# First layer of a two-layer Hedgehog-attention and Mish kernel: six blocks' normalized rows are turned by VectorE and reloaded from DRAM by features; the first stage's products run by kinds

## The chip, the cores and the metric

The kernel runs on one NeuronCore of one Trainium2 chip. The metric is the device time of one execution in microseconds (us), lower is better. Engines are named TensorE (PE in the profile, with PEld for its weight loads), VectorE (DVE), ScalarE (ACT), GpSimd (POOL) and SyncE (SP, which issues the DMAs). PSUM is the memory that TensorE writes; the other tiles lie in SBUF.

## What is computed

Two equal layers over x of 2048 rows and 640 features, in fp32. The layers share their weights.

```python
x = A_x                                           # (1, 2048, 640)
for layer in range(2):
    x = x + A(layernorm(x)) ; x = x + B(layernorm(x))

def A(x):                                         # linear attention, 32 heads of 20
    q, k, v = split(x @ wqkv)
    pq, pk = q @ w_phi, k @ w_phi                 # per head, 20 x 20
    phi = concat(softmax(p), softmax(-p))         # of pq and of pk, 40 wide
    kv, z = phi_k^T v, sum over rows of phi_k
    return ((phi_q kv) / (phi_q z + 1e-6)) @ wo
def B(x):                                         # 640 -> 1536 -> 640
    h = x @ w1 + b1
    return (h * tanh(softplus(h))) @ w2
```

## The kernel before

The 2048 rows are cut in NB = 8 blocks of 256 rows, each of BT = 2 tiles of 128 rows; NT = 16 tiles in all. A product in fp32 precision is made of three TensorE matmuls in a rounded format (fp32r): every operand is kept as a high part (ScalarE copies it to the rounded format) and a low part (VectorE subtracts the high part from the original), and high x high, high x low and low x high are accumulated in PSUM.

Each layer has three stages. The first stage (`attend_first`) makes queries, keys and values of every tile and accumulates phi_k^T [v, 1] over all rows. The second stage (`attend_second`) applies that to the queries, multiplies by wo, adds the result to the rows and takes their statistics. The third (`dense`) is the Mish layer.

The change lies in the first stage. Its matmuls need the normalized rows with the features on the partitions, that is transposed. In the first layer, `fetch_normed(b)` loads a block of rows (line 384), takes mean and variance (`norm_stats`, VectorE lines 250 and 252; `norm_scale`, GpSimd lines 259 and 260, VectorE line 262), `normed` writes the normalized rows to two row tiles (ScalarE, by `act`), and `Transposed.step` turns them on TensorE: a block has 5 x 2 squares of 128 x 128, ten transposes through PSUM (line 280). The same `step` then makes high and low parts (lines 285 and 286; three steps of four, four and two squares). In the second layer the end of `dense` has already normalized the rows; `spill_turned` transposes them on VectorE within 32 x 32 blocks (line 315) and writes them with eight DMAs of 80 KB (line 317) to a DRAM tensor laid out by features, n2_d; `fetch_normed` there only calls `load_turned`, three loads into row tiles (line 325), and `step` makes the parts straight from these tiles, without TensorE. `dense` gets its own inputs by the same route, through n1_d.

For each tile there are three products of 30 matmuls (line 344): keys, queries and values, written k0, q0, v0 for the block's first tile and k1, q1, v1 for its second. `order` gives their sequence, by blocks. Each is a generator: its first part computes the product and moves it out of PSUM, and each later call of `advance`, once per product, takes every pending generator one part further, newest first. For keys the parts are:

- right after the product: ScalarE moves it out of PSUM to a "big" tile
- one product later: VectorE takes maxima and minima (line 368, two), and makes both differences (lines 369 and 371)
- two later: ScalarE's exponential
- three later: VectorE's sums and reciprocals (lines 377 and 378), GpSimd's scaling (line 379)
- five later: 22 matmuls accumulate phi_k^T [v, 1] (line 414)

Queries go the same way, with line 369 on GpSimd, into a tile of their own ring ("r" in the profile, two tiles); four products later VectorE transposes them in 32 x 32 blocks (line 423) and four DMAs of 160 KB write them to e_d, by features (line 427). Values are only moved out of PSUM.

Between the products of block b, at index n of the order, block b+1 is prepared: at n = 0 `fetch_normed(b + 1)`, at n = 2 `normed`, and at n = 3, 4 and 5 one `step` each.

A scheduler orders the instructions of every engine from this program by a simulated timeline; `act` ties ScalarE's instructions of this stage in program order. Buffers: product tiles in PSUM ("mm") 2, other PSUM tiles ("one") 4, "big" 5, rows ("xt") 2, row tiles ("xn") 4, values ("v") 2.

Of the kernel before, what the change touches and what calls it, by code (L numbers as in the profile page):

```python
# [18 lines left out]
D = 640  # L19
# [5 lines left out]
BT = 2  # L25
# [17 lines left out]
def kernel(  # L43
# [56 lines left out]

    e_d = [dram.tile([EW, BLK], F32, name=f"e_d{b}") for b in range(NB)]

    n1_d = [dram.tile([D, BLK], F32, name=f"n1_d{b}") for b in range(NB)]
    n2_d = [dram.tile([D, BLK], F32, name=f"n2_d{b}") for b in range(NB)]
    x1_d = dram.tile([S, D], F32, name="x1_d")
# [140 lines left out]
    def norm_stats(t, xt):  # L246

        bn = work.tile([P, 2, 6], F32, tag="bn", name="bn", bufs=2)
        for c in range(2):
            nc.vector.bn_stats(bn[:, c], xt[:, t, c * HC:(c + 1) * HC])  # L250
        mv = work.tile([P, 2], F32, tag="mv", name="mv", bufs=3)
        nc.vector.bn_aggr(mv, bn)
        return mv

    def norm_scale(b, mvs):

        ve = work.tile([P, BT], F32, tag="ve", name="ve", bufs=2)
        for t in range(BT):
            nc.gpsimd.tensor_scalar(ve[:, t:t + 1], mvs[t][:, 1:2], LN_EPS, 1.0, op0=ALU.add, op1=ALU.mult)
        nc.gpsimd.tensor_tensor(stats[:, b, 0], ve, neg_half, op=ALU.pow)  # L260
        for t in range(BT):
            nc.vector.scalar_tensor_tensor(stats[:, b, 1, t:t + 1], mvs[t][:, 0:1], -1.0,
                                           stats[:, b, 0, t:t + 1], op0=ALU.mult, op1=ALU.mult)
# [35 lines left out]
    def normed(b, xt):  # L299

        xn = [row_tile() for _ in range(BT)]
        for t in range(BT):
            act(xn[t], xt[:, t, :], AF.Identity,
                                 bias=stats[:, b, 1, t:t + 1], scale=stats[:, b, 0, t:t + 1])
        return Transposed(xn)
# [13 lines left out]
    def load_turned(src, tiles):  # L319

        cols = []
        for c, make in zip(range(0, KD, 2), tiles):
            n = min(2, KD - c)
            cols.append(make()[:, :n * BLK].rearrange("p (k s) -> p k s", k=n))
            nc.sync.dma_start(cols[-1], src[c * P:(c + n) * P].rearrange("(k p) s -> p k s", p=P))
        return Transposed(cols=cols)
# [55 lines left out]
    def fetch(x_src, b, xt=None):  # L382
        xt = x_tile() if xt is None else xt
        nc.sync.dma_start(xt, row_block(x_src, b))
        return xt

    def attend_first(layer, x_src, first):


        def fetch_normed(b):  # L390
            if layer:
                return load_turned(n2_d[b], [row_tile] * 3)
            xt = fetch(x_src, b)
            norm_scale(b, [norm_stats(t, xt) for t in range(BT)])
            return xt

        pending = []

        def advance():
            for g in pending[::-1]:  # L400
                try:
                    next(g)
                except StopIteration:
                    pending.remove(g)

        def keys(xts, i, v):
            e = big_tile()
            yield from features(project(xts, i % BT, kv_ws, 0), e, False)
            yield
            for g in range(G):  # L410
                p, n = divmod(g, 2)
                w, m = (120, 64) if g < 10 else (80, 42)
                acc, c = (kva, 120 * p) if p < 4 else (kvz, 120 * (p - 4))
                nc.tensor.matmul(acc[64 * n:64 * n + m, c:c + w], v[:, GW * g:GW * g + m],  # L414
                                 e[:, 120 * g:120 * g + w],
                                 start=(i == 0 and p in (0, 4)), stop=(i == NT - 1),
                                 skip_group_check=True)

        def queries(xts, i, ps=None):
            e = query_tile(i)  # L420
            yield from features(project(xts, i % BT, q_ws, 0) if ps is None else ps, e, True)

            nc.vector.transpose(e, e)
            b, t = divmod(i, BT)
            dst = e_d[b].rearrange("(j f) (t q s) -> t q f j s", f=32, t=BT, s=32)
            for q in range(4):
                nc.sync.dma_start(dst[t, q], e[32 * q:32 * q + 32].rearrange("f (j s) -> f j s", s=32))
                if b == NB - 1:
                    yield

        def values(xts, i, v):
            vv = v.rearrange("p (h d) -> p h d", d=DH + 1)
            act(vv[:, :, DH], ident[:, :H], AF.Copy, scale=0.0, bias=1.0)
            if i < BT:
                pv = project(xts, i, kv_ws, D, [one_tile(), one_tile()])
                for c in range(2):
                    act(vv[:, c * H // 2:(c + 1) * H // 2, :DH],
                        pv[c][:, :HC].rearrange("p (h d) -> p h d", d=DH), AF.Copy)
            else:
                pv = project(xts, i % BT, kv_ws, D)  # L440
                act(vv[:, :, :DH].rearrange("p (c h) d -> p c h d", c=2),
                    both(pv).rearrange("p c (h d) -> p c h d", d=DH), AF.Copy)
            yield

        if first is None:
            with tc.manual_schedule(engines={mybir.EngineType.SP}):
                bd = big_tile()[:120, :720].rearrange("p (t c) -> p t c", t=6)
                nc.sync.dma_start(bd[:, :3], phi_bd[:, :3])
                raw = load_raw(0, range(3))
                xt = fetch_normed(0)  # L450
                nc.sync.dma_start(bd[:, 3:], phi_bd[:, 3:])
                raw += load_raw(0, range(3, 6))
                nxt = normed(0, xt).all()
                q_ws = [r2_pair(k) for k in range(KD)]
                fold_phi(q_ws, bd, raw)
                kv_ws = load_v_weights()
                raw = load_raw(1)
            nc.sync.dma_start(mask, head_mask)
        else:
            nxt, kv_ws = first  # L460
            q_ws = load_q_weights()
        for b in range(NB):
            xts = nxt
            order = ("k0", "v0", "q0", "k1", "v1", "q1")
            if b == 0:
                order = ("v0", "q0", "v1", "k0", "q1", "k1")
            elif b == 1:
                order = ("k0", "q0", "k1", "v0", "q1", "v1")
            elif b == NB - 1:
                order = ("k0", "k1", "v0", "v1", "q0")  # L470
            vs = [v_tile() for _ in range(BT)]
            for n, (kind, t) in enumerate(order):
                t = int(t)
                i = b * BT + t
                if b == 0 and n == 1:
                    if layer:
                        load_k_weights(kv_ws)
                if b == 0 and n == 3:
                    if layer == 0:
                        fold_phi(kv_ws, bd, raw)  # L480
                    kva, kvz = one_tile(), one_tile()
                if b == NB - 1 and n == 3:
                    loaded = {0: load(0)}
                if b + 1 < NB:
                    if n == 0:
                        xt = fetch_normed(b + 1)
                    elif n == 2:
                        nxt = xt if layer else normed(b + 1, xt)
                    elif n > 2:
                        nxt.step()  # L490
                g = {"k": lambda: keys(xts, i, vs[t]), "q": lambda: queries(xts, i),
                     "v": lambda: values(xts, i, vs[t])}[kind]()
                next(g)
                advance()
                pending.append(g)
            if b == 1:
                if layer == 0:
                    spill_qk_weights(kv_ws, q_ws)
                o_ws = load_o_weights()

        def rest():

            ps = [one_tile(), one_tile()]
            project_half(ps[0], xts, 1, q_ws, 0, 0)
            advance()
            advance()
            yield
            project_half(ps[1], xts, 1, q_ws, 0, 1, range(3))
            yield
            project_half(ps[1], xts, 1, q_ws, 0, 1, range(3, KD))  # L510
            pending.append(queries(xts, NT - 1, ps))
            next(pending[-1])
            while pending:
                yield
                advance()

        return kva, kvz, o_ws, loaded, rest()
# [379 lines left out]
```

## Time and profile before

| | us |
|---|---|
| median of 3 runs (1401.17 to 1402.03) | 1401.89 |
| the profiled execution | 1400.33 |
| its span, first to last instruction | 1398.6 |
| TensorE busy | 1384.2 |
| VectorE busy | 1074.5 |
| ScalarE busy | 584.1 |
| GpSimd busy | 442.3 |
| granted TensorE clock | 1.000 |

The profile names an instruction by its line in the kernel, its engine, its operation and `out<-in` by the program's tile names. In a table of groups, "x4 | 3.0, 801 | 0.4 <-ACT" means four instructions, 3.0 us busy in all, 801 ns for one on average, and 0.4 us in which the engine stood idle before them, ended by ScalarE. A row of a timeline is start, duration, engine, line, operation and the number of instructions merged in it. A row of waits names who waited for whom, the total, the number of times and the longest. A row of the chain of waits is start, length, engine, line and count. Consecutive matmuls overlap in the pipeline, so their distance from start to start is shorter than one's duration.

The first layer's first stage runs until about 281 us, its blocks 1 to 6 from 53 to 237 us; the second layer's first stage lies around 715 to 960 us.

### The profile page before, as it was taken

The page shows a single profiled execution, that of the slowest core. Times are in us where ns is not written, and L with a number is a line of the kernel's source. Part 1 is how long each engine was busy: PE and PEld are TensorE (multiplying, and loading weights), DVE is VectorE, ACT ScalarE, POOL GpSimd, SP SyncE. Part 2 cuts the span into 40 slices and gives each one's busy share as a digit, 9 for nine tenths or more (in the row PEclk, how much of TensorE's full clock was granted, in tenths as well). Part 3 has the DMA queues.
Part 4 walks back from the last instruction along what each step waited for, and adds up shares of the span by engine and source line. Part 5 has one row for each costly group of instructions (what it writes and reads, how often), then busy time and mean ns, then how long its engine had stood idle before and what let it go on. Part 6 is the DMA issues. An engine that isn't in the chain of part 4 may idle for free. (4 is left out here: it accounts for less than half of the span.)

```text
span 1398.6 us, 28120 instructions
## 1 busy us (share of the span) xinstructions
PE 1384.2 (99%) x11528; PEld 1367.6 (98%) x11528; DVE 1074.5 (77%) x1820; ACT 584.1 (42%) x973; POOL 442.3 (32%) x334
## 2 busy tenths in 40 slices
PE   7999999999999999999999999999999999999998
PEld 7999999999999999999999999999999999999998
DVE  5798877696698877788769887887767876767775
ACT  4444344321355454545454333332234444444443
POOL 1354444343422222222234443433352211211112
PEclk9999999999999999999999999999999999999999
DMA  8533422689733423343374333357976212333200
GB/s 319 169 79 57 75 40 39 185 237 292 254 87 95 111 75 64 91 114 95 106 273 89 71 65 69 50 109 218 288 251 208 69 26 77 95 95 95 73 24 20
DMA packets 350035, 169.57 MB, mean 121 GB/s; under 512 B 286866, under 2 KB 323458, under 8 KB 349906
## 3 DMA queue, kind: packets, MB, share of 16 engines
q1 hardware_dynamic: 349906, 167.78, 44.2%
q8 instruction: 90, 1.47, 0.4%
q14 instruction: 39, 0.32, 0.1%
HBM read 104.82 MB, written 62.91 MB: 120 GB/s over the span
## 5 line engine op out<-in xcount | busy, mean ns | idle before, releaser
L735 PE MATMUL mm<-r2h,ol 128*128 128x320 f32 x1280 | 304.7, 309 | 0.0
L719 POOL TENSOR_TENSOR ol<-big,ol 128x512 fp32r<-128x512 f32 (+1 forms) x98 | 129.8, 1325 | 484.1 <-ACT ol L718 407.8
L693 PE MATMUL one<-xtl,r1h 128*128 128x256 f32 x960 | 268.2, 279 | 0.0
L693 PE MATMUL one<-xth,r1l 128*128 128x256 f32 x960 | 268.0, 279 | 0.0
L693 PE MATMUL one<-xth,r1h 128*128 128x256 f32 x960 | 265.9, 279 | 0.0
L735 PEld LDWEIGHTS mm<-r2h,ol 128*128 128x128 f32 x1280 | 219.1, 188 | 0.0
L735 PE MATMUL mm<-r2l,ol 128*128 128x320 f32 x640 | 197.3, 309 | 0.0
L344 PE MATMUL mm<-r1h,xth 128*128 128x320 f32 x600 | 188.3, 314 | 0.0
L344 PE MATMUL mm<-r1h,xtl 128*128 128x320 f32 x600 | 185.7, 310 | 0.7 <-DVE xtl L286 0.7
L344 PE MATMUL mm<-r1l,xth 128*128 128x320 f32 x600 | 185.6, 309 | 0.0
L693 PEld LDWEIGHTS one<-xtl,r1h 128*128 128x128 f32 x960 | 180.4, 188 | 0.0
L693 PEld LDWEIGHTS one<-xth,r1l 128*128 128x128 f32 x960 | 180.4, 188 | 0.0
L693 PEld LDWEIGHTS one<-xth,r1h 128*128 128x128 f32 x960 | 179.6, 188 | 0.0
L708 DVE TENSOR_SCALAR big<-big 128x512 f32<-128x512 f32 (+1 forms) x98 | 56.4, 575 | 110.7 <-ACT big L706 110.5
L379 POOL TENSOR_TENSOR r<-r,r 128x1280 f32<-128x1280 f32 x32 | 75.8, 2367 | 142.6 <-DVE r L378 136.8
L735 PEld LDWEIGHTS mm<-r2l,ol 128*128 128x128 f32 x640 | 120.2, 188 | 0.0
L710 ACT ACTIVATE big<-big,two 128x512 f32<-128x512 f32 (+1 forms) x98 | 70.1, 715 | 116.1 <-DVE big L709 116.1
L706 ACT ACTIVATE big<-one,b1s 128x256 f32<-128x256 f32 x192 | 80.8, 467 | 90.2 <-PE one L693 89.7
L718 ACT ACTIVATE ol<-big 128x512 fp32r<-128x512 f32 (+1 forms) x98 | 61.0, 622 | 135.8 <-DVE big L717 135.7
L344 PEld LDWEIGHTS mm<-r1h,xth 128*128 128x128 f32 x600 | 112.8, 188 | 2.0
L344 PEld LDWEIGHTS mm<-r1h,xtl 128*128 128x128 f32 x600 | 112.8, 188 | 1.1 <-DVE xtl L286 1.0
L344 PEld LDWEIGHTS mm<-r1l,xth 128*128 128x128 f32 x600 | 112.8, 188 | 0.0
(129 smaller groups left out, 3158.1 us busy)
## 6 DMA issues: line engine op xcount, KB each, us to landing
e_d<-r SPq DMA_DIRECT2D x128, 160.0 KB, 4.0
big<-e_d SPq DMA_DIRECT2D x32, 640.0 KB, 6.8
x_d<-xt SPq DMA_DIRECT2D x23, 640.0 KB, 4.1
xt<-x_d SPq DMA_DIRECT2D x22, 640.0 KB, 4.4
n_d<-xn SPq DMA_DIRECT2D x176, 80.0 KB, 2.1
xt<-in_x SPq DMA_DIRECT2D x16, 640.0 KB, 5.7
xn<-x_d SPq DMA_DIRECT2D x28, 320.0 KB, 4.6
v<-n_d SPq DMA_DIRECT2D x30, 256.0 KB, 2.9
```

Of the source, the lines that this page charges most:

```text
L344: nc.tensor.matmul(ps[:, :HC], a[:, sl], r, start=(k == 0 and n == 0), stop=(k == KD - 1 and n == 2))
L379: nc.gpsimd.tensor_tensor(eg, eg, r.unsqueeze(2).to_broadcast([P, 2 * H, DH]), op=ALU.mult)
L693: nc.tensor.matmul(ph[:, j, :], l, r, start=(n == 0), stop=(n == 3 * KD - 1))
L706: exps[0] = nc.scalar.activation(part(ta, 0)[:, j - js.start], ph[:, j, :], AF.Exp, bias=b1s[:, 2 * pr + j:2 * pr + j + 1]).ins
L708: nc.vector.tensor_scalar_min(e, e, E_CAP)
L710: nc.scalar.activation(r, n, AF.Ln, bias=two)
L718: nc.scalar.activation(ah[:, js], n, AF.Copy)
L719: nc.gpsimd.tensor_tensor(al[:, js], n, ah[:, js].bitcast(F32), op=ALU.subtract)
L735: nc.tensor.matmul(pys[t][:, c, :HC], l[:, j, sl], r, start=(f == 0 and n == 0), stop=(f == KF - 1 and n == 2))
```

## The change

Blocks 2 to 7 of the first layer take the second layer's route. A new generator `turn(b)` fetches block b, takes its statistics and, at its second call, normalizes the rows in place in the fetched tile and hands them to `spill_turned`, which transposes them on VectorE and writes them to a new DRAM tensor, n0_d. It is called for block b + 2 while block b is computed, at n = 1 and n = 3. `fetch_normed(b + 1)`, at n = 0 of block b, then is `load_turned` from n0_d for these blocks, and the loaded tiles are used directly. Blocks 0 and 1 stay as they were.

In both layers, the order of blocks 2 to 6 becomes k0 k1 v0 v1 q0 q1 (blocks 0, 1 and 7 keep theirs), and the first tile's keys of blocks 2 to 6 wait one `advance` longer before their accumulation.

```diff
+    n0_d = [dram.tile([D, BLK], F32, name=f"n0_d{b}") for b in range(NB)]
...
+        def turned(b):
+            return layer or b > 1
+        def turn(b):
+            xt = fetch(x_src, b)
+            norm_scale(b, [norm_stats(t, xt) for t in range(BT)])
+            yield
+            rows = [xt[:, t, :] for t in range(BT)]
+            normalize(b, rows, rows)
+            spill_turned(rows, n0_d[b])
+            yield
         def fetch_normed(b):
-            if layer:
-                return load_turned(n2_d[b], [row_tile] * 3)
+            if turned(b):
+                return load_turned((n2_d if layer else n0_d)[b], [row_tile] * 3)
...
             yield from features(project(xts, i % BT, kv_ws, 0), e, False)
             yield
+            if i % BT == 0 and BT < i < NT - BT:
+                yield
...
-            order = ("k0", "v0", "q0", "k1", "v1", "q1")
+            order = ("k0", "k1", "v0", "v1", "q0", "q1")
...
                     elif n == 2:
-                        nxt = xt if layer else normed(b + 1, xt)
+                        nxt = xt if turned(b + 1) else normed(b + 1, xt)
...
+                if not layer and b + 2 < NB:
+                    if n == 1:
+                        ahead = turn(b + 2)
+                        next(ahead)
+                    elif n == 3:
+                        next(ahead)
```

## The prediction

> **What bounds the kernel now.** First the head of the page and TensorE's waits over the whole span, to see whether any engine but TensorE sets the end.
>
> ```profile
> span 1398.6 us, 28120 instructions
> ...
> PE 1384.2 (99%) x11528; PEld 1367.6 (98%) x11528; DVE 1074.5 (77%) x1820; ACT 584.1 (42%) x973; POOL 442.3 (32%) x334
> ```
>
> ```profile
> PE mm L237 <- DMA raw<-in_wqk_t: 7.9, 3, 4.2
> ...
> PE mm L344 <- DVE xtl L286: 0.7, 1, 0.7
> PE one L414 <- POOL big L379: 0.4, 1, 0.4
> ```
>
> TensorE is busy 1384.2 of 1398.6 us, and most of what it waits is for the first weights. So time is gained only by giving TensorE fewer instructions, and lost only where something else makes it wait. The change gives it fewer in the first layer's first stage. What one block costs there, and what the same block costs without transposes, is read off TensorE's timeline (first layer) and the chain of waits (second layer, whose turned rows already come from DRAM).
>
> ```profile
> 164.07 1.38 PE L414 MATMUL one<-big,v 128*64 128x120 f32 x22
> 165.38 0.66 PE L280 MATMUL one<-ident,xn 128*128 128x128 f32 x4
> ...
> 194.54 1.38 PE L414 MATMUL one<-big,v 128*64 128x120 f32 x22
> ```
>
> ```profile
> 831.31 1.31 PE one L414 x22
> 832.62 13.40 PE mm L344 x90
> ...
> 860.72 1.31 PE one L414 x22
> ...
> 966.59 1.09 PE one L280 x10
> ```
>
> From one accumulation to the same one a block later is 194.54 - 164.07 = 30.47 us in the first layer and 860.72 - 831.31 = 29.41 us in the second. The difference, 1.06 us, is the ten L280 transposes of a block (ten take 1.09 us in the chain). One product of 30 matmuls is 13.40 / 3 = 4.47 us; six, with two accumulations of 1.31, make the 29.41.
>
> Then the table by stage: blocks 1 to 6 of the first layer, the second layer's first stage while its VectorE is behind (740 to 775), and one steady block of it.
>
> ```profile
> 53.48:85.40 31.92, 31.92 (x247) 31.40 (x245) 31.17 (x37) 15.25 (x20) 17.55 (x10) 1.00 0.41 84
> 85.40:115.00 29.60, 29.60 (x232) 28.86 (x230) 27.05 (x41) 10.93 (x18) 17.47 (x13) 1.00 0.38 70
> 115.00:145.40 30.40, 30.40 (x236) 29.78 (x235) 25.68 (x35) 12.09 (x18) 12.57 (x7) 1.00 0.37 66
> 145.40:175.87 30.47, 30.47 (x236) 29.85 (x235) 25.39 (x36) 12.16 (x18) 14.06 (x10) 1.00 0.36 66
> 175.87:206.34 30.47, 30.47 (x236) 29.85 (x235) 24.46 (x30) 12.17 (x18) 13.43 (x9) 1.00 0.30 44
> 206.34:236.80 30.46, 30.46 (x236) 29.84 (x235) 23.51 (x27) 12.16 (x18) 11.95 (x6) 1.00 0.30 45
> 740.00:775.00 35.00, 34.55 (x272) 33.55 (x271) 35.00 (x35) 14.49 (x19) 18.72 (x9) 1.00 0.38 71
> 831.24:860.65 29.41, 29.41 (x226) 28.81 (x225) 23.86 (x27) 10.53 (x15) 12.30 (x6) 1.00 0.38 68
> ```
>
> Columns: stretch, its length, then busy time of PE, PEld, DVE, ACT, POOL, the granted clock, DMA share, GB/s. TensorE has no gap in blocks 1 to 6, at full clock. VectorE is the next engine: 31.17 of 31.92 us in block 1 and about 25 of 30.5 later. The change adds work to this engine, so the question is whether it stays behind TensorE.
>
> **What is removed: 60 transposes.** Blocks 2 to 7, ten each: 6 x 1.06 = **-6.4 us** on TensorE, all on the path.
>
> **What is added on VectorE.** The groups of one first-layer block (145.40 to 175.87), then the same line in a second-layer block, then the turning as the dense stage shows it:
>
> ```profile
> L368 DVE TENSOR_REDUCE m<-big 128x32 f32<-128x640 f32 x4 | 3.0, 801 | 0.4 <-ACT big L116 0.4
> L423 DVE STREAM_TRANSPOSE r<-r 128x1280 f32<-128x1280 f32 x2 | 3.0, 1498 | 0.0
> ...
> L377 DVE TENSOR_REDUCE r<-big 128x64 f32<-128x1280 f32 x2 | 3.0, 1475 | 0.0
> L369 DVE TENSOR_TENSOR big<-big,m 128x640 f32<-128x640 f32 x2 | 2.5, 1246 | 0.0
> L371 DVE TENSOR_TENSOR big<-m,big 128x640 f32<-128x640 f32 x3 | 2.5, 825 | 0.1
> L378 DVE RECIPROCAL r<-r 128x64 f32<-128x64 f32 x4 | 2.2, 546 | 0.0
> L250 DVE BATCH_NORM_STATS2 bn<-xt 128x6 f32<-128x320 f32 x4 | 1.7, 478 | 0.0
> ...
> L286 DVE TENSOR_TENSOR xtl<-one,xth 128x512 fp32r<-128x512 f32 x2 | 1.3, 669 | 0.0
> L286 DVE TENSOR_TENSOR xtl<-one,xth 128x256 fp32r<-128x256 f32 x1 | 0.4, 416 | 0.0
> L252 DVE BATCH_NORM_AGGREGATE mv<-bn 128x2 f32<-128x12 f32 x2 | 0.4, 176 | 0.0
> ```
>
> ```profile
> L286 DVE TENSOR_TENSOR xtl<-xn,xth 128x512 fp32r<-128x512 f32 x2 | 2.4, 1210 | 0.0
> ...
> L286 DVE TENSOR_TENSOR xtl<-xn,xth 128x256 fp32r<-128x256 f32 x1 | 0.4, 415 | 0.0
> ```
>
> ```profile
> L315 DVE STREAM_TRANSPOSE xn<-xn 128x640 f32<-128x640 f32 x44 | 36.3, 833 | 2.2 <-ACT xn L116 2.1
> ```
>
> Two transposes a block: 2 x 0.833 = 1.67 us. The low halves are now taken from a loaded tile instead of PSUM: 2 x (1.210 - 0.669) = 1.08 us more. Together 2.75 us a block. The row statistics stay, only a product earlier and a block further ahead. A full block comes to 25.39 + 2.75 = 28.1 us of VectorE against 29.41 of TensorE: it fits, with 1.3 us to spare.
>
> Block by block (blocks 1 to 3 without their ten transposes; statistics counted where they are now): block 1 has 31.17 + 2.75 = 33.9 us of VectorE against 31.92 - 1.06 = 30.9 of TensorE, 3.0 behind; block 2 has 29.8 against 28.5, 4.3 behind; block 3 28.4 against 29.3, 3.4; block 4 28.1 against 29.4, 2.1; block 5 27.2 against 29.4, none. So VectorE is **up to 4.4 us later** than today at the end of block 2, and full through blocks 1 to 3 (30.9 + 28.5 + 29.3 = 88.7 us). Bounds of what this costs TensorE: below, 0, since block 1 had VectorE at 31.17 of 31.92 and TensorE without a gap; above, the whole 4.4, once, for a wait of TensorE lets VectorE catch up. The nearest row is 740 to 775: same stage, turned rows from DRAM, VectorE 35.00 of 35.00, and TensorE lost 35.00 - 34.55 = 0.45 us. I take that rate: 0.45 / 35 x 88.7 = **+1.1 us**.
>
> **The order by kinds, in both layers, blocks 2 to 6.** Nothing is added, but VectorE's jobs bunch. A key product brings 2 x 0.801 + 1.246 + 0.825 = 3.7 us one product later and 1.475 + 0.546 = 2.0 us three products later; a query product 2.4, 2.0 and, four later, 1.5 (L423). With k0 k1 v0 v1 q0 q1 and the turning (statistics 2.1 at the second product, transposes at the fourth), with the low halves in the last three, the six products bring 2.4, 7.8, 7.2, 5.8, 3.2 and 2.8 us (29.2; rows overlap a little at their ends, so the block's 28.1 is less). Against 4.47 each (7.1 in the first, with both accumulations) VectorE is 3.3 us behind after the second product, then 6.1, 7.4, 6.1, 4.4, and 0 after the next block's first. k1's second job is then over (7.4 + 1.2 + 2.0 after the fifth product's start) 1.7 us into the next block's first product; GpSimd's scaling (2.37 us, below) ends at 4.1, and the accumulation, held for both keys by the extra wait line to the end of that product, is due at 4.47. That covers it by 0.4 us in the first layer; in the second layer, where statistics and turning are left out of the same sum, by 4.1 us. I put the order at **0**: what it costs where that cover fails is the lateness already bounded at 4.4. The extra wait holds a fourth "big" tile of five for one product more, which blocks nobody.
>
> **DMAs.** Each block adds eight spills and three loads to SP's queue.
>
> ```profile
> n_d<-xn SPq DMA_DIRECT2D x176, 80.0 KB, 2.1
> ...
> xn<-n_d SPq DMA_DIRECT2D x14, 256.0 KB, 3.2
> ```
>
> ```profile
> 428.99 4.38 SPq L317 DMA_DIRECT2D n_d<-xn  x8
> ```
>
> Issue 4.4 us, landing 2.1, three load issues at 0.55 (1.6), landing 3.2. Counted from the fourth product's end plus 7.4 us of lateness that is 18.7 us; the halves are first taken 2 x 4.47 + 7.1 + 2 x 4.47 = 25.0 us after it, and TensorE needs them 13.4 us later still. Behind these issues on SP stand the queries' spills and the next row fetch; the queue works about 4.4 + 1.6 us more in 29.4. DMA engines are at a 0.36 share. Cost **0**; if the cover were gone, see the third rival.
>
> **Sum.** -6.4 + 1.1 = -5.2 us (unrounded -6.36 + 1.14). The profiled execution took 1400.33 us, 1.7 more than its span of 1398.6 and 1.6 under the median 1401.89: its span would be 1393.4, its time 1395.1, and the median **1396.7**.
>
> A rule speaks against the move. The Trainium skill, VectorE: DVE Perf Modes, section "Rules for kernel authors", advises TensorE for a 128x128 transpose whose result may go to PSUM. Its table's 390 ns for one would make 60 of them 23.4 us (an estimate from that page); the chain's 1.09 us for ten decides, and the sum keeps 6.4.
>
> **Rivals.**
> 1. *The lateness turns into waits in full*: the accumulations of blocks 2 and 3 wait for GpSimd's scaling, 4.4 us in all. -6.4 + 4.4 = -2.0: 1399.9. For it: only 0.4 us of cover. Against: TensorE ran gapless at 98% VectorE.
> 2. *VectorE becomes the bound*, slower. Two of its operands in SBUF, and it waits for GpSimd:
>
> ```profile
> 821.66 0.65 DVE L286 TENSOR_TENSOR xtl<-xn,xth 128x512 fp32r<-128x512 f32 x1
> ...
> 824.82 1.77 DVE L286 TENSOR_TENSOR xtl<-xn,xth 128x512 fp32r<-128x512 f32 x1
> ```
>
> ```profile
> 823.67 2.37 POOL L379 TENSOR_TENSOR big<-big,r 128x1280 f32<-128x1280 f32 x1 [3.71 <-DVE r L378]
> ```
>
> The second ran into GpSimd's 2.37 us and took 1.12 us longer. A block has eight such operations (two L369, four L371, two L286). From 1.3 us more a block, little over one such hit, VectorE decides. Two more hits make 28.1 + 2.2 = 30.3 against 29.4: 0.9 x 6 = 5.4, and the 4.4 of lateness is never won back: -6.4 + 5.4 + 4.4 = +3.4, 1405.3. Against: the turning itself reads one operand, and the present blocks already hold some hits. The Trainium skill, SBUF — State Buffer, section "Who interferes with whom", states the same as an exclusive lock, for a VectorE instruction with two SBUF inputs against a GpSimd instruction that reads SBUF; the trace agrees (1.77 against 0.65 us), and the low halves move under that rule here.
> 3. *The round trip through DRAM is late*, so the change doesn't do what it says: TensorE waits at each turned block's start. It decides beyond 25.0 + 13.4 - 18.7 = 20 us of extra delay; at 21 us the 1.06 of each block is gone: 1401.9. Little speaks for it.
>
> **How the numbers follow.** Forecast 0.65, rival 1 0.14, rival 2 0.15, rival 3 0.06. This kernel's measurement tells 0.2% (2.8 us) from no change: below 1399.1 is faster, above 1404.7 slower. The forecast is faster; rival 1, just inside, I split 0.03 faster and 0.11 same; rival 3 is same; rival 2 slower. Faster 0.68, same 0.17, slower 0.15. The forecast's own range is 1395.5 (no wait) to 1399; low end 1394.5, with the runs' 0.9 us of spread; the high end 1404.5 holds rivals 1 and 3 and stops short of rival 2.
>
> **What would show it.** L280 in the first layer's first stage falls from 80 to 20 and a steady block there measures 29.4 us. VectorE's row reads near 28 of 29.4, full through blocks 1 to 3. TensorE's waits for L379 and L286 stay near 1 us in total; 4 us there shows rival 1, a block over 30.3 us with VectorE full rival 2, waits on a DMA or on L286 at block starts rival 3. Second-layer blocks stay at 29.41; if they don't, the order was mispriced.

## The result, and the profile after

| | before | after |
|---|---|---|
| median, us | 1401.89 | 1409.44 (1408.29 to 1411.84, 5 runs) |
| ratio to before, 95% interval | 1 | 1.0057 (1.0046 to 1.0069) |
| the profiled execution | 1400.33 | 1409.64 |
| its span | 1398.6 | 1407.8 |

The kernel became 7.5 us slower; 1396.7 was predicted, 5.2 us faster. First the head of the page of the changed kernel and TensorE's waits over its whole span, without those for the first weights (who waited for whom, total us, times, longest).

```profile
span 1407.8 us, 28150 instructions
...
PE 1379.7 (98%) x11468; PEld 1363.4 (97%) x11468; DVE 1097.8 (78%) x1832; ACT 584.0 (41%) x973; POOL 443.2 (31%) x334
```

```profile
...
PE one L431 <- POOL big L380: 5.3, 5, 2.4
PE mm L345 <- DVE xtl L287: 3.1, 4, 1.2
PE mm L345 <- ACT v L117: 2.0, 1, 2.0
PE mm L345 <- DVE r1l L244: 2.0, 1, 2.0
PE mm L345 <- ACT r L117: 1.5, 2, 0.9
```

TensorE has 60 matmuls fewer, the transposes, and is busy 4.5 us less; the span is 9.2 us longer all the same. Before, TensorE waited 1.1 us for GpSimd's scaling and the low halves together, after 5.3 + 3.1, and waits on ScalarE and on the key weights' low parts are new. (Line numbers have moved: L344 is now L345, L414 L431, L423 L440, L427 L444, L315 L316, L317 L318, L286 L287, L250 L251, L368 L369, L369 L370, L371 L372, L379 L380, L384 L385; L244 makes the low parts of the folded weights. In the experiments' kernels the numbers differ by a few lines again.)

The table by stage of the changed kernel shows where. Columns as in the prediction: stretch, length, busy time of PE, PEld, DVE, ACT, POOL, granted clock, DMA share, GB/s. From 133.85 us on a stretch is a whole block, from the end of one pair of accumulations to the end of the next.

```profile
40.00:55.07 15.07, 13.12 (x91) 12.56 (x91) 9.13 (x18) 6.02 (x10) 2.61 (x4) 1.00 0.92 260
55.07:85.14 30.07, 28.10 (x204) 27.51 (x202) 26.63 (x36) 14.22 (x19) 18.34 (x12) 1.00 0.39 108
85.14:110.00 24.86, 21.47 (x162) 20.25 (x162) 23.30 (x29) 7.50 (x11) 12.72 (x8) 0.86 0.72 136
...
133.85:166.45 32.60, 29.94 (x226) 28.78 (x224) 24.97 (x34) 11.29 (x17) 12.65 (x8) 1.00 0.55 107
166.45:197.33 30.88, 29.48 (x226) 28.77 (x224) 25.76 (x37) 11.32 (x17) 14.60 (x9) 1.00 0.56 105
197.33:228.10 30.77, 29.41 (x224) 28.77 (x225) 26.76 (x30) 12.76 (x19) 12.40 (x6) 1.00 0.52 88
228.10:257.17 29.07, 29.07 (x226) 28.77 (x224) 27.16 (x31) 10.99 (x16) 13.44 (x7) 1.00 0.40 72
```

Two different losses are in it. Up to 110 us TensorE idles 1.95 + 1.97 + 3.39 us, and its clock drops to 0.86 in the mean of one stretch. Then three whole blocks take 32.60, 30.88 and 30.77 us, in which VectorE is busy only 25 to 27 us: it isn't full, it stands idle for 4 to 8 us of each. The last block, 29.07 us, has no gap, and is shorter than the 29.41 us that the prediction expected.

The second layer gained. The chain of waits of the changed kernel (start, length, engine, line, count):

```profile
844.77 2.47 PE one L431 x43
847.24 26.60 PE mm L345 x180
873.84 2.47 PE one L431 x43
```

A block there takes 873.84 - 844.77 = 29.07 us, against 29.41 before. The two accumulations of a block now stand side by side, and TensorE changes over between the two kinds of matmul once a block less: 180 matmuls of the products in a row take 26.60 us, where two runs of 90 took 2 x 13.40, and the accumulations together 2.47 in place of 2 x 1.31.

What TensorE waited for up to 110 us (timeline of TensorE in the changed kernel; in brackets the idle time before the instruction and who ended it):

```profile
45.18 0.41 PE L345 MATMUL mm<-r1h,xth 128*128 128x320 f32 x1 [1.95 <-DVE r1l L244]
...
85.14 0.41 PE L345 MATMUL mm<-r1h,xth 128*128 128x320 f32 x1 [1.98 <-ACT v L117]
...
92.19 0.41 PE L345 MATMUL mm<-r1h,xth 128*128 128x320 f32 x1 [0.89 <-ACT r L117]
...
96.02 2.52 PE L431 MATMUL one<-big,v 128*64 128x120 f32 x22 [2.39 <-POOL big L380]
```

The causes of the first stand in VectorE's timeline, of the second in ScalarE's:

```profile
42.46 1.66 DVE L316 STREAM_TRANSPOSE xt<-xt 128x640 f32<-128x640 f32 x2
...
44.69 0.88 DVE L244 TENSOR_TENSOR r1l<-mm,r1h 128x280 fp32r<-128x280 f32 x2
...
74.23 2.98 DVE L370 TENSOR_TENSOR big<-big,m 128x640 f32<-128x640 f32 x1
...
87.57 2.85 DVE L287 TENSOR_TENSOR xtl<-xn,xth 128x512 fp32r<-128x512 f32 x1
```

```profile
80.97 1.28 ACT L117 ACTIVATE big<-big 128x1280 f32<-128x1280 f32 x1 [4.70 <-DVE big L372]
...
82.67 1.72 ACT L117 ACTIVATE xt<-xt,stats 128x640 f32<-128x640 f32 x2
...
84.41 0.68 ACT L117 ACTIVATE v<-mm 128x640 f32<-128x640 f32 x1
```

At 42.46 us the turning of block 2, whose products come only after the next block's, stands before the low parts of the key weights (L244), which TensorE needs at once. The last two rows are hits beside GpSimd: 2.98 and 2.85 us for operations whose means in the prediction's rows are 1.246 and 1.210. At 80.97 ScalarE had waited 4.70 us for a VectorE that was full, and then normalized the next block to be turned (1.72 us) before it moved the value product out of PSUM, at 84.41, for which TensorE stood still.

For the steady blocks, one block of the changed kernel: SP's timeline, then VectorE's, then ScalarE's.

```profile
179.65 3.31 SPq L444 DMA_DIRECT2D e_d<-r  x4
184.44 4.33 SPq L318 DMA_DIRECT2D n_d<-xt  x8
188.86 3.51 SPq L444 DMA_DIRECT2D e_d<-r  x4
```

```profile
183.58 1.56 DVE L316 STREAM_TRANSPOSE xt<-xt 128x640 f32<-128x640 f32 x2
...
185.50 1.45 DVE L440 STREAM_TRANSPOSE r<-r 128x1280 f32<-128x1280 f32 x1
...
197.31 1.55 DVE L369 TENSOR_REDUCE m<-r 128x32 f32<-128x640 f32 x2 [4.90 <-ACT r L117]
```

```profile
196.58 0.70 ACT L117 ACTIVATE r<-mm 128x640 f32<-128x640 f32 x1 [9.45 <-DMA e_d<-r]
```

The reader is to follow one query tile through three engines. VectorE turns the block's row tiles (183.58) and only then the second query's features (185.50, done at 186.95). Their spill goes out on SP from 188.86, behind the eight row spills (184.44 to 188.77): 1.9 us late by that queue alone. When it has landed, the next block's second query may be moved out of PSUM: the ring has two tiles. ScalarE, whose instructions are tied in program order, has stood 9.45 us for that, and VectorE 4.90 us for ScalarE. It is a loop, closed by way of DRAM: by ScalarE's timeline the second query is moved out at 164.85 and again at 196.58, a round of 31.7 us, where TensorE needs 29.07 for a block. The waits of ScalarE and VectorE on DMAs, 40 to 260 us; first in the kernel before, then after, where two views give a row each:

```profile
ACT r L116 <- DMA e_d<-r: 3.3, 1, 3.3
```

```profile
ACT r L117 <- DMA e_d<-r: 50.3, 10, 9.4
```

```profile
DVE bn L251 <- DMA xt<-in_x: 8.1, 4, 3.7
```

The last row is a second new wait: VectorE stands before the statistics of rows that have not landed, and the work that follows on VectorE starts after them.

### The profile page after: what moved, and what is told of

Same layout as the page of the kernel before. It is cut to its first block, busy times and chain, and to the rows that moved or that the text cites. A ratio compares the mean times of both kernels' runs of the same rounds, so it can differ in the third digit from the quotient of the medians.

```text
span 1407.8 us, 28150 instructions
## 1 busy us (share of the span) xinstructions
PE 1379.7 (98%) x11468; PEld 1363.4 (97%) x11468; DVE 1097.8 (78%) x1832; ACT 584.0 (41%) x973; POOL 443.2 (31%) x334
## 5 line engine op out<-in xcount | busy, mean ns | idle before, releaser
L345 PE MATMUL mm<-r1h,xth 128*128 128x320 f32 x600 | 188.0, 313 | 5.6 <-ACT v L117 2.0
L345 PE MATMUL mm<-r1h,xtl 128*128 128x320 f32 x600 | 186.7, 311 | 3.2 <-DVE xtl L287 3.1
L345 PE MATMUL mm<-r1l,xth 128*128 128x320 f32 x600 | 186.2, 310 | 0.0
L345 PEld LDWEIGHTS mm<-r1h,xth 128*128 128x128 f32 x600 | 113.4, 189 | 8.0 <-ACT r L117 2.3
L380 POOL TENSOR_TENSOR r<-r,r 128x1280 f32<-128x1280 f32 x32 | 76.9, 2403 | 130.5 <-DVE r L379 122.6
L345 PEld LDWEIGHTS mm<-r1h,xtl 128*128 128x128 f32 x600 | 113.2, 189 | 4.8 <-DVE xtl L287 4.5
L345 PEld LDWEIGHTS mm<-r1l,xth 128*128 128x128 f32 x600 | 113.4, 189 | 0.0
```

What stands on the lines that cost most here:

```text
L345: nc.tensor.matmul(ps[:, :HC], a[:, sl], r, start=(k == 0 and n == 0), stop=(k == KD - 1 and n == 2))
L380: nc.gpsimd.tensor_tensor(eg, eg, r.unsqueeze(2).to_broadcast([P, 2 * H, DH]), op=ALU.mult)
```

## The experiments

Every kernel ran beside the kernel before on the same chip (its medians: 1401.41 to 1402.02). For all of them the place of one instruction is compared: the first matmul of the first accumulation pair that stands as one run of 44 matmuls, and the same three blocks later (the old order has no such run). In the kernel after, by TensorE's timeline:

```profile
131.38 2.54 PE L431 MATMUL one<-big,v 128*64 128x120 f32 x44
...
225.63 2.54 PE L431 MATMUL one<-big,v 128*64 128x120 f32 x44 [0.75 <-POOL big L380]
```

| kernel | median, us | ratio to before, 95% | pair at | three blocks take |
|---|---|---|---|---|
| after | 1409.44 | 1.0046 to 1.0069 | 131.38 | 94.25 |
| order alone | 1399.13 | 0.9968 to 0.9987 | 123.20 | 90.53 (with transposes) |
| old order, turning | 1411.03 | 1.0039 to 1.0072 | | |
| no turning at all | 1393.00 | 0.9917 to 0.9950 | 121.70 | 87.21 |
| no spills | 1402.22 | 0.9994 to 1.0013 | 130.45 | 89.77 |
| no 32x32 transposes | 1405.41 | 1.0016 to 1.0035 | 127.09 | 94.04 |
| turning later | 1404.19 | 1.0008 to 1.0027 | 128.04 | 92.27 |
| fetch earlier | 1410.71 | 1.0043 to 1.0073 | 130.80 | 94.34 |
| both | 1403.47 | 1.0002 to 1.0021 | 127.93 | 91.12 |
| both, statistics tied | 1397.81 | 0.9960 to 0.9984 | 126.87 | 87.20 |
| early and tied, turning not later | 1409.68 | 1.0031 to 1.0070 | 128.86 | 96.79 |
| after, from block 4 on | 1399.50 | 0.9975 to 0.9994 | 124.02 | 93.06 |
| all three, from block 4 on | 1393.74 | 0.9931 to 0.9956 | 123.30 | 87.21 |

The pair can itself slip against the products around it: without spills the three distances are 33.39, 27.31 and 29.07 us. So the split into start and blocks is good to about 1 us.

### The order alone

The kernel before, with the new order and the longer wait of the first key:

```diff
+            if i % BT == 0 and BT < i < NT - BT:
+                yield
...
-            order = ("k0", "v0", "q0", "k1", "v1", "q1")
+            order = ("k0", "k1", "v0", "v1", "q0", "q1")
```

> The kernel before with the order by kinds and the extra wait line alone, nothing turned. Theory 'queue' (the second query tile's spill stands on SP behind the eight spills of the turned rows, and ScalarE waits for that tile) and theory 'VectorE' (the added work makes VectorE late) both expect no change: 1402 us, 1400.5 to 1403.5, TensorE without gaps in blocks 2 to 6. Theory 'order' (the bunching by itself makes TensorE wait) expects 1405 or more, with waits in both layers.

Measured 1399.13 against 1401.78: 2.65 us faster, which none of the three theories expected. Five blocks in each layer have the new order; 10 x 0.34 would be 3.4 us, so the shorter blocks can carry it. The order is a gain of its own, and no part of the loss.

### The turning with the old order

The reverse of that diff, on the kernel after.

> The changed kernel with the order of before and without the extra wait line; turning kept. The order alone gained 2.7 us. If the two parts only add: 1412. If the order by kinds is what the turned rows' work collides with (both queries adjacent): 1406 or below.

Measured 1411.03, 1.6 us slower than after. Going back to the old order repairs nothing: the loss comes with the turning in either order.

### No turning at all

In the kernel after, blocks 2 to 7 are neither fetched, normalized, turned nor spilled ahead; the three loads take as many bytes of the input instead, so the output isn't the reference's.

```diff
         def turn(b):
-            xt = fetch(x_src, b)
-            norm_scale(b, [norm_stats(t, xt) for t in range(BT)])
             yield
-            rows = [xt[:, t, :] for t in range(BT)]
-            normalize(b, rows, rows)
-            spill_turned(rows, n0_d[b])
             yield
```

> The changed kernel without statistics, normalizing, turning and spills of blocks 2 to 7: the loads take the input's bytes instead, so the rows of these blocks are not normalized. 60 transposes fewer and no added work but the loads. 'queue' and 'VectorE': 1401.9 - 6.4 = 1395.5, up to 1397; steady first-layer blocks at 29.4 us. 'order': 1399 or more.

Measured 1393.00. Against the order alone this is 1399.1 - 1393.0 = 6.1 us: the 60 transposes were worth what the prediction said (6.4). Against after it is 16.4 us: that is what the turning work costs, where the prediction had 1.1. By the table it falls into two parts, 131.38 - 121.70 = 9.7 us ahead of the first pair and 94.25 - 87.21 = 7.0 us in the three blocks behind it. ScalarE waits for the query tile here too, 26.1 us between 40 and 260 us, some 4 us in each of the later blocks, and TensorE has no gap in them: waits of that length cost nothing here; those of after reach 8 to 9 us.

### Turning without spills, spills without turning

```diff
-            spill_turned(rows, n0_d[b])
+            for t in range(BT):
+                nc.vector.transpose(rows[t], rows[t])
```

(the loads again take the input's bytes), and on the other side, with all DMAs in place,

```diff
-            nc.vector.transpose(rows[t], rows[t])
+            if turning:
+                nc.vector.transpose(rows[t], rows[t])
```

with `turning` false for these blocks. The outputs of both are not the reference's.

> The changed kernel with statistics, normalizing and turning kept, but without the 48 spills of turned rows: the loads take the input's bytes, so blocks 2 to 7 use rows that are not normalized. 'queue': blocks 3 to 5 fall from 32.6, 30.9 and 30.8 to 29.4 us and the time to 1404 or below (5.4 us of TensorE's idle time there goes; the waits at 45 and at 83 to 102 us may stay). 'VectorE': its work is the same, so 1408 or more.

> The changed kernel without the twelve VectorE transposes of the turned rows (the rows are normalized and spilled unturned): 10 us less of VectorE's work in blocks 0 to 5, DMAs as in the changed kernel. 'load': 1403 or below. 'fetch' and 'queue': 1406 to 1410.

Without the 48 spills 7.2 us come back, without the twelve transposes 4.0 us, of 16.4. Neither is the cause alone. The split by place says more: without spills the three blocks take 89.77 in place of 94.25 us and the start is almost as late as in after (130.45); without VectorE's transposes the start is 4.3 us earlier (127.09), and the blocks take 94.04, of which some 1.5 us are a stretch at a lower granted clock (0.96 and 0.99 in the means of 130 to 160 and 160 to 190 us). So the start suffers mostly from work on the engines, the blocks mostly from the DMAs. ScalarE's wait for the query tile, 50.3 us in after and 26.1 without any turning, falls in both, to 27.8 and 33.0 us: each takes something from in front of the second query's spill, the one on SP, the other on VectorE. (1405.41, without the transposes, lies between what the theories expected.)

### Turning later, rows earlier, and both

The normalizing, turning and spilling moved from the fourth product to the sixth, so that the spills stand behind the second query's, and the fetch and the statistics to the first and the third:

```diff
-                    if n == 1:
+                    if n == 0:
                         ahead = turn(b + 2)
                         next(ahead)
-                    elif n == 3:
+                    elif n in (2, 5):
```

> The changed kernel with the same work, only moved: rows fetched at the first product of a block, statistics at the third, normalizing and turning at the sixth, so that the turned rows' spills follow both query spills on SP. 'queue': blocks at 29.4 to 29.8 us, the time 1404 or below. 'VectorE': same work, 1407 or more, blocks over 30.5 us.

The rows fetched a block earlier, the turning where it was:

```diff
-            xt = fetch(x_src, b)
+            xt = early.pop(b) if b in early else fetch(x_src, b)
...
+                if not layer and b + 3 < NB and n == 4:
+                    early[b + 3] = fetch(x_src, b + 3)
```

> The changed kernel with the row fetch of a block to be turned issued one block earlier; nothing else moved. Theory 'fetch' (VectorE, in order, stands before the statistics until the rows have landed: 8.1 us in four waits of the changed kernel, and what comes after is late by that): those waits go and the time falls to 1404 or below. Theory 'queue' (spills of turned rows before the second query's spill) or 'load' (VectorE has too much to do): 1407 or more.

The early fetch, and the turning at the sixth product (`elif n == 5`), the statistics staying at the second:

> The early fetch of the run before, and normalizing, turning and spilling at the sixth product instead of the fourth, so that the spills follow both query spills. If 'fetch' and 'queue' together make the loss in steady blocks: blocks 3 to 5 at 29.1 to 29.5 us and 1401 or below, with the waits of blocks 0 to 2 left. 'load': 1404 or more, as VectorE's work is unchanged.

Turning later gave 1404.19, 5.2 us better than after; ScalarE's wait for the query tile fell from 50.3 to 24.7 us, but a block still took 30.8 us, not the 29.4 to 29.8 expected. The earlier fetch gave 1410.71, nothing, and did not test what it was meant to. VectorE's wait on the rows in that kernel:

```profile
DVE bn L251 <- DMA xt<-in_x: 7.4, 3, 4.7
```

The wait had not gone, because the fetch had not moved. One fetch on SP in after, then the same one in the kernel with the earlier fetch:

```profile
132.77 0.43 SPq L385 DMA_DIRECT2D xt<-in_x  x1
```

```profile
131.50 0.43 SPq L385 DMA_DIRECT2D xt<-in_x  x1
```

The next goes out at 164.60 and 164.43 us, and the statistics stand right behind the landing in both kernels (at 138.24 and 136.69). The rows have two tiles, and in after this fetch comes 3.9 us after the last issue of the eight spills that empty a tile (123.29 to 128.92), so there was hardly room for an earlier one; no run with a third tile shows it. With both (1403.47) the wait was still there, 4.5 us in two waits, and a block took 30.4 us: more than the 1401 expected, and not clearly better than turning later alone.

### Statistics tied behind VectorE's newest maxima

The kernel with both, and with the statistics kept behind the newest features' maxima. All six blocks are turned and everything is computed.

```diff
-            nc.vector.tensor_reduce(m[:, s], eh[:, 1], axis=AX.X, op=op)
+            newest[0] = nc.vector.tensor_reduce(m[:, s], eh[:, 1], axis=AX.X, op=op).ins
...
-            norm_scale(b, [norm_stats(t, xt) for t in range(BT)])
+            with (tc.issue_after(newest[0]) if newest[0] else ExitStack()):
+                norm_scale(b, [norm_stats(t, xt) for t in range(BT)])
```

> Early fetch, late turning, and the statistics tied behind VectorE's newest maxima, so that the scheduler can't put them where the rows have not landed. Theory 'fetch': its waits on the rows (4.5 us in the kernel with early fetch and late turning, median 1403.5) go and 1400 or below follows. 'load' or 'queue' alone: no change, 1402.5 to 1404.5.

Measured 1397.81: 11.6 us better than after, 3.6 better than before. The table by stage of this kernel for the first and the third of the three blocks, and SP's timeline between:

```profile
126.87:155.94 29.07, 29.07 (x226) 28.77 (x225) 27.02 (x37) 12.15 (x17) 13.39 (x10) 1.00 0.62 117
...
185.00:214.07 29.07, 29.07 (x225) 28.77 (x224) 27.59 (x38) 12.26 (x17) 13.18 (x10) 1.00 0.54 93
```

```profile
168.14 11.42 SPq L448 DMA_DIRECT2D e_d<-r  x8
182.33 5.13 SPq L319 DMA_DIRECT2D n_d<-xt  x8
```

Both queries' spills now go out ahead of the row spills, and TensorE has no gap. The fetch still goes out where it did (159.97 us for the last block); what the tie moved is the statistics, which start a block later (at 186.37 us, where after has 170.28), and VectorE waits for no rows any more between 40 and 260 us. VectorE does the same work as in after, 27.0 and 27.6 us of 29.07, more of the block than in after's slow ones: it was never short of throughput here. At the start 126.87 - 121.70 = 5.2 us are still lost.

### Early and tied, with the turning left at the fourth product

This tells the wait on the rows from the place of the turning, and with it the order of SP's queue: the kernel just shown with `elif n == 3` again. The normalizing on ScalarE and the turning on VectorE move along with the spills.

> As the kernel after, with rows fetched one block earlier and the statistics of the turned blocks tied behind VectorE's newest maxima; normalizing, turning and the eight spills stay at the fourth product, so the second query's four spills still stand behind them on SP. Two theories of the 1.5 to 2 us that a steady block loses: (fetch) VectorE standing before rows that have not landed makes the features late, and the queue only passes that on: without that wait the three blocks after 130 us take 29.1 to 29.5 us each, ScalarE's waits for the query tile fall below 15 us between 40 and 260 us, and the time is 1402 to 1404 (the ramp's waits stay). (queue) the second query's spills behind the eight row spills are enough by themselves: blocks stay above 30 us, ScalarE's waits for the tile stay near 50 us, and the time is 1406 to 1410 although VectorE no longer waits on rows.

Measured 1409.68: the theory of the fetch falls, and that of the queue holds in the main. The three blocks take 96.79 us, of which some 3.4 are a stretch at half clock (shown at the end); the first of them takes 29.07, the next two 32.78 and 34.94. VectorE has no wait on rows left between 40 and 260 us, and ScalarE still waits, if less than the 50 us expected:

```profile
ACT r L118 <- DMA e_d<-r: 40.4, 7, 9.5
```

SP's timeline has the order of after again:

```profile
175.48 3.29 SPq L448 DMA_DIRECT2D e_d<-r  x4
180.47 4.26 SPq L319 DMA_DIRECT2D n_d<-xt  x8
184.83 3.45 SPq L448 DMA_DIRECT2D e_d<-r  x4
```

Turned later, without the tie, it is 1403.47; with the tie, not later, 1409.68; with both 1397.81. With the turning at the fourth product, the tie changes nothing that can be told (1410.71 without it, 1409.68 with it); where the queue is in order, it is worth 5.7 us. No run moves the spills alone. That the spills are the larger part of it rests on the run without them, where normalizing and turning stayed at the fourth product and 4.5 of the blocks' 7.0 us came back.

### From block 4 on

The kernel after with only blocks 4 to 7 turned; blocks 2 and 3 keep their twenty transposes on TensorE.

```diff
-            return layer or b > 1
+            return layer or b > 3
...
-                if not layer and b + 2 < NB:
+                if not layer and 3 < b + 2 < NB:
```

> The changed kernel with blocks 4 to 7 turned instead of 2 to 7, so that no turning falls in blocks 0 and 1. Theory 'ramp' (the losses before 110 us, 7.3 us of idle TensorE and a halved clock for 6.8 us, come from turning work put where VectorE is full already): they go, 20 transposes (2.1 us) come back, 1403 or below; steady blocks as in the changed kernel. If the loss only moves to the first block that turns: 1407 or more.

The same with the early fetch, the tie and the later turning:

> Blocks 4 to 7 turned, rows fetched a block earlier, statistics tied, turning at the sixth product. If ramp and steady losses have separate causes and all are met: the order alone (1399.1) less 4 x 1.06, so 1395, up to 1397. If turning costs what it saves even so: 1399 or more.

Leaving blocks 2 and 3 alone gave 1399.50, 9.9 us better than after although TensorE does twenty transposes more (2.1 us): turning these two blocks cost 12.0 us. The start is whole again (124.02 is 121.70 + 2.1 + 0.2), and the slow blocks are all there (93.06 us; ScalarE's wait for the query tile 51.3 us). The other three edits then take 5.8 us more, 1393.74: the three blocks fall from 93.06 to 87.21. This version is faster than both kernels, 0.57% under before (0.44 to 0.69%). Head of its page, and TensorE's largest wait from 20 us on:

```profile
span 1391.6 us, 28141 instructions
...
PE 1377.4 (99%) x11488; PEld 1363.6 (98%) x11488; DVE 1090.4 (78%) x1828; ACT 584.7 (42%) x973; POOL 441.2 (32%) x334
```

```profile
PE mm L600 <- PE mm L600: 0.9, 2, 0.4
```

## Why the prediction was wrong, point by point

- *60 transposes, -6.4 us.* Right: 6.1 us between the order alone and no turning at all.
- *The order at 0.* Mispriced on the good side: -2.65 us. The prediction counted two accumulations as 2 x 1.31 us and six products as 6 x 4.47 wherever they stand; side by side they take 2.47 and 26.60, and a block 29.07 in place of 29.41. Its own test for this ("Second-layer blocks stay at 29.41") found it.
- *VectorE late by up to 4.4 us, +1.1.* This step failed first, for 9.7 us. It summed VectorE's work by block and took what a full VectorE had cost elsewhere, 0.45 us in 35. The sum did not ask what stands at the moment right behind the new work. It begins at block 1, but block 2's turning falls into block 0: VectorE is busy only 9.13 of 15.07 us there, and TensorE still waited 1.95 us, because the key weights' low parts stood behind the turning. Nor was VectorE full where TensorE lost the rest (26.63 of 30.07 and 23.30 of 24.86 us). The waits of 1.95, 1.98, 0.89 and 2.39 us exceed the bound of 4.4 us (the block sums add up to 4.3), which was argued from "a wait of TensorE lets VectorE catch up": the waits were not for VectorE alone (VectorE, ScalarE twice, GpSimd), and the lower clock behind them, some 3.4 us, was in no term. That these blocks are the cause is shown by leaving them out (12.0 us); which of the four waits is worth how much was not tried singly.
- *The DMAs at 0.* This step failed second, in the blocks' 7.0 us. The prediction saw what was behind the eight spills on SP ("the queries' spills and the next row fetch") and counted only how long the queue works. It had to ask how late that makes the second query's spill, and who waits for it: a ring of two tiles, and with it ScalarE in program order. Without the spills the blocks win 4.5 of the 7.0 us back (89.77). With the turning late, and so the queue in order, they win 3.1 back (91.12); with the statistics tied as well, all of it (87.20); and with the turning back at its place none (96.79).
- *"The row statistics stay, only a product earlier and a block further ahead."* Costed at nothing. VectorE spent 8.1 us in front of rows on their way. Undone with the queue as it was, this gave nothing; with the queue in order it gave the other 3.9 us of the blocks and 1.1 at the start.
- *Rival 1*, at 14%, had the mechanism of the start in part (waits for GpSimd's scaling), at 4.4 us where the start lost 9.7. *Rival 2* had the sign: VectorE as the bound by its throughput. It is refuted for the steady blocks, where VectorE idles 4 to 8 us of each and does as much work in 29.07 us once it isn't made to wait. In the start, the long hits beside GpSimd that it rested on do occur (2.98 and 2.85 us); no run separates them from the rest of the start's loss.
- *Rival 3*, the turned rows late at TensorE, did not happen: TensorE waits for no load of theirs. What came late by way of DRAM was the query, a transfer that was there before.

The end of it in one sum of differences between medians, which add up by construction: -2.65 (order) - 6.1 (transposes) + 16.4 (turning: 9.7 at the start and 7.0 in the blocks by the traces, 0.3 more than the medians) = +7.6. The split between start and blocks is the part that the traces add.

## What to carry to other kernels

Adding work to an engine or a queue with room to spare can still lengthen a loop that has little: look for rings of tiles whose release goes by a DMA, add up the round (eviction, features, transposing, spill, landing), compare it with a block, and put new DMAs behind the spill that closes it. New work of a block far ahead has to be kept out of the first blocks here, where what TensorE needs at once stands right behind it, and its instructions may have to be tied behind what is urgent: by its simulated times the scheduler had put the statistics right behind their fetch, where VectorE stood 8.1 us. And an edit that moves a fetch says nothing until the trace shows that the transfer moved.

## What was not expected of the hardware

TensorE's granted clock fell after short waits. In the kernel with early, tied statistics and the turning at the fourth product, TensorE's timeline reads:

```profile
214.99 0.30 PE L346 MATMUL mm<-r2l,xth 128*128 128x320 f32 x1
215.14 0.31 PE L346 MATMUL mm<-r2h,xtl 128*128 128x320 f32 x1
217.11 0.41 PE L346 MATMUL mm<-r1h,xth 128*128 128x320 f32 x1 [1.67 <-ACT r L118]
...
223.12 0.47 PE L346 MATMUL mm<-r1h,xth 128*128 128x320 f32 x1
223.38 0.47 PE L346 MATMUL mm<-r1l,xth 128*128 128x320 f32 x1
```

The matmuls start 0.15 us apart before the wait and 0.26 to 0.27 us apart from about 218.7 to 225.5 us, after a wait of 1.67 us with some 24 us free of waits ahead of it (one of 0.17 us came at 218.6). In the changed kernel the same happens between 95 and 102 us (the stretch with a granted clock of 0.86), after waits of 1.98, 0.89 and 2.39 us within 11 us; at half speed for 6.8 us this costs 3.4 us, a third of the loss at the start. Yet its wait of 1.95 us at 45 us left the clock at 1.00, while in the kernel with the earlier fetch the same instruction waited the same 1.95 us, at 45.08, and the mean granted clock from 40 to 50 us was 0.83. A longer wait left the clock alone in the kernel with all six blocks turned late and tied, whose granted clock is 1.000 throughout; its row of TensorE's waits:

```profile
PE mm L346 <- DVE xtl L288: 3.0, 2, 2.3
```

The Trainium skill, TensorE: Matmul & The Clock Gate, section "HAM oscillation — how this bites in real kernels", puts the limit at idle gaps of about 3.4 us. No gap of TensorE in these stretches is as long, so the measurement decides: 1.67 us was enough in one place, and 2.3 us was not in another. Since the same wait of 1.95 us did it in one kernel and not in the other, the length of a wait alone doesn't decide; what is counted stays open, and no run was made for it. The price in these traces is a wait's own length and 1.7 us (the 0.83 in the mean of 10 us) or 3.4 us more.
